# A decode step in fp32: weight rows added on DVE instead of multiplied on PE, shorter programs, the last parts of DVE and PE placed in front

## The chip, the cores and the metric

The kernel runs on one core of a Trainium2 chip. The metric is device time in microseconds (us). The engines are called as the profile calls them: PE (TensorE, with PEld for its weight loads), DVE (VectorE), ACT (ScalarE), POOL (GpSimd) and SP (SyncE, which issues nearly all DMAs here). A name with a q (SPq, PEq) is that engine's sequencer.

## The reference

One token passes through attention over a cache and a gated feed-forward layer, side by side; both results are added to the input. All is float32.

```python
# x (1,1,576); k_cache, v_cache (1,32,16384,128); wq (576,4096); wo (4096,576)
# w_gate, w_up (576,4608); w_down (4608,576)
xn = _layernorm(x)
q = xn @ wq                                  # 32 heads of 128
p = softmax(einsum(q, k_cache) * 128**-0.5)  # per head, over 16384 keys
attn = concat_heads(p @ v_cache) @ wo
h = gelu(xn @ w_gate) * (xn @ w_up)
out = x + attn + h @ w_down
```

## The kernel before

The keys and values of one head are one tile each, 128 partitions x 16384 floats (8.39 MB): partition p holds 128 keys of 128 floats. SBUF holds three such slots: two for K (`kt`, used by even and odd heads) and one for V (`vt`). The weights use the same slots before the heads start and w_down and wo after they end.

`Plan` keeps one list of operations for each engine (`q`). `op` adds one with the semaphores that it waits for, and on DVE, ACT and POOL each operation also waits for the one before it on its engine; `dma` adds a load with its own semaphore; `call` adds a function that writes its instructions itself, which is how loops get in. `emit` writes an engine's list in order, and leaves out waits that an earlier one covers. `take` waits for a semaphore and lowers it again. The order on each engine is the order of the calls in `plan`.

1. x is normalised on one partition and spread over 128 partitions by five small matmuls (L206, L207): partition p gets entries 4p to 4p+3 of xn (`xp`), and the last 64 entries go to two partitions each (`xt`).
2. `wide` (L214) multiplies on PE: the weight rows are the moving operand, `xnb` (xn repeated 32 times) the stationary one. wq takes 40 matmuls, gate and up 60 each. `select` (L237) picks on DVE, for each partition, the columns that belong to it out of the PSUM result, by a product with a mask and a reduction: `qsel` for q, `gu` for gate and up. The gelu (L264 to L269) runs on DVE with one tanh on ACT and gives `hT`.
3. For each of 32 heads: PE spreads the head's q to all partitions (L287), ACT copies it to `qb`; DVE multiplies the K tile with it in place (`products`, L308) and sums over 128 floats (`sums`, L312), takes the maximum through PE (L315 to L317); ACT does the exponentials (L347); PE multiplies them with the V tile in 32 matmuls (L296); ACT and PE gather the result (L349, L301, L351). The first two heads of DVE stand ahead of its loop, the first K tile in two halves.
4. SP issues the loads one by one from a list of 62 (`load_k`, `load_v`): a K load waits for DVE's sums of the head two before (`s_kf`), a V load for PE's use of the V before (`s_vf`). The first K loads wait for PE to be done with gate and up (`done`).
5. `down` (L378) adds the 36 rows of w_down on DVE into `wacc`: 28 (`wd0`) and 5 (`AHEAD`) before the softmax sums are gathered to `oT` (L400 to L406), 3 after. Of wo's 32 rows DVE adds 8 (`ON_DVE`), PE multiplies 18 into `acc` and the last 6 into `fin` (`out_rows`, L413); `part` = `acc` + `wacc` is summed over partitions into `fin` too, which began with x (L419). Each of the last seven rows of wo is a load of its own.

Of the kernel before, what the change touches and what calls it, by code (L numbers as in the profile page):

```python
# [24 lines left out]
FQ = DF // 4  # L25
WT = HD // P
CUT = ((0, 11), (11, 22), (22, 32))
# [5 lines left out]
ON_DVE = range(8)  # L33
AHEAD = 5
LAST = 6


class Plan:
# [26 lines left out]

    def call(self, e, fn):
        self.q[e].append((None, fn, None, 0))

    def emit(self, e, g, seen, ops):
        for deps, fn, sig, by in ops:  # L70
            if deps is None:
                fn(g)
                continue
            need = {}
            for s, n in (d for d in deps if d):
                if n > max(seen.get(s.name, 0), need.get(s.name, (s, 0))[1]):
                    need[s.name] = s, n
            for k, (s, n) in need.items():
                g.wait_ge(s, n)
                seen[k] = n  # L80
            made = fn(g)
            if made is not None:
                made.then_inc(sig, by)

    def run(self, ahead):
        seen = {e: {} for e in self.NAMES}
        for e, n in ahead.items():
            self.emit(e, getattr(self.nc, self.NAMES[e]), seen[e], self.q[e][:n])
        with self.nc.Block(no_gpsimd_drain=True) as block:
            for e, name in self.NAMES.items():  # L90
                getattr(block, name)(lambda g, e=e: self.emit(e, g, seen[e], self.q[e][ahead.get(e, 0) :]))
# [12 lines left out]
def plan(nc, pl, x, k_cache, v_cache, wq, wo, wg, wu, wd, out):  # L104
# [31 lines left out]
    xnb, xtb = small("xnb", [P, DJ, 32]), small("xtb", [P, 2, 32])  # L136
# [7 lines left out]
    tmp = small("tmp", [P, 32 * FT])  # L144
    over = place["tmp"]
    xn, xd = small("xn", [1, D], over), small("xd", [1, D - DM, 2], over + 4 * D)
    t1, th, t2 = (small(f"t{i}", [P, FT], over + 160 * i) for i in range(3))
# [4 lines left out]
    A, B, C = 0, SLOT, 2 * SLOT  # L152
    wqm, wqt = big("wqm", DJ * HD, A), big("wqt", HD // 2, B)
    gm, gt = big("gm", DJ * DF, B + 8192), big("gt", DF // 2, B + 8192 + 16 * DF)
    ua, ub, ut = big("ua", 2 * DF, B + 8192 + 18 * DF), big("ub", 2 * DF, A), big("ut", DF // 2, A + 8 * DF)
# [9 lines left out]
    pqs, pg, pu = banks(("pqs", 2), ("pg", 3), ("pu", 3))  # L165
    po, pqb, pt, pb, pc, acc, fin = banks(("po", 1), ("pqb", 1), ("pt", 1), ("pb", 1), ("pc", 1), ("acc", 2), ("fin", 1))
    px = pu[:, 0, :]
# [41 lines left out]
    k_xnb = op("dve", lambda g: g.tensor_copy(xnb, xp[:, :DJ].unsqueeze(2).to_broadcast([P, DJ, 32])), k)  # L209
    k = op("dve", lambda g: g.tensor_scalar(xt, par, xp[:, DJ:], None, op0=ALU.mult), k, c_par)  # L210
    k_x = op("dve", lambda g: g.tensor_copy(xtb, xt.unsqueeze(2).to_broadcast([P, 2, 32])), k)


    def wide(dst, b, cols, pieces, t, tcols):  # L214
        n = cols[1] - cols[0]
        k = None
        for j in range(DJ + 1):
            for i in range(4):
                o = dst[32 * i : 32 * i + 32, b, :n]
                if j < DJ:  # L220
                    w, dep = pieces[j]
                    c = i * tcols
                    args = xnb[:, j, :], w[:, c + cols[0] : c + cols[1]]
                else:
                    w, dep = t
                    c = (i % 2) * tcols
                    args = xtb[:, i // 2, :], w[:, c + cols[0] : c + cols[1]]
                k = op("pe", lambda g, o=o, a=args, j=j: g.matmul(o, *a, start=j == 0, stop=j == DJ), dep, k_x)  # L228
        return k

    rows = [(wqm[:, j * HD : (j + 1) * HD], d_q[0]) for j in range(DJ)]
    for b in range(2):
        k_q = wide(pqs, b, (512 * b, 512 * b + 512), rows, (wqt, d_q[1]), HD // 4)
    d_ub = dma("sp", ub, main["u"][:, 2 * DF :], k_q)
    d_ut = dma("sp", ut, tail["u"], k_q)

    def select(view, dst, r):  # L237
        tv = tmp[:, : r * dst.shape[-1]].rearrange("p (r t) -> p r t", r=r)
        k = None
        for lo, hi, src, dep in view:  # L240
            k = op("dve", lambda g, lo=lo, hi=hi, src=src: g.tensor_mul(  # L241
                tv[:, lo:hi, :], src.rearrange("p (r t) -> p r t", r=hi - lo),
                m32[:, lo:hi].unsqueeze(2).to_broadcast([P, hi - lo, dst.shape[-1]])), dep, c_m32)
        return op("dve", lambda g: g.tensor_reduce(dst, tv.rearrange("p r t -> p t r"), axis=AX.X, op=ALU.add), k)

    k_qs = select([(0, 8, pqs.rearrange("p b f -> p (b f)"), k_q)], qsel, 8)

    gp = [(gm[:, j * DF : (j + 1) * DF], d_g[j // 2]) for j in range(DJ)]
    up = [(ua[:, :DF], d_ua), (ua[:, DF:], d_ua), (ub[:, :DF], d_ub), (ub[:, DF:], d_ub)]
    done = []  # L250
    for i, (dst, pieces, t) in enumerate(((pg, gp, (gt, d_g[2])), (pu, up, (ut, d_ut)))):
        view = []
        for b, (lo, hi) in enumerate(CUT):
            k = wide(dst, b, (FT * lo, FT * hi), pieces, t, FQ)
            view.append((lo, hi, dst[:, b, : FT * (hi - lo)], k))
        done.append(k)
        k_f = select(view, gu[:, i, :], 32)

    for z in (po, acc, fin):
# [3 lines left out]
    g_, u_ = gu[:, 0], gu[:, 1]  # L263
    k = op("dve", lambda g: g.tensor_mul(t1, g_, g_), k_f)  # L264
    k = op("dve", lambda g: g.tensor_scalar(t1, t1, 0.044715, 1.0, op0=ALU.mult, op1=ALU.add), k)
    k = op("dve", lambda g: g.tensor_mul(t1, t1, g_), k)
    k = op("act", lambda g: g.activation(th, t1, AF.Tanh, scale=0.7978845608028654), k)
    k = op("dve", lambda g: g.scalar_tensor_tensor(t2, th, 1.0, g_, op0=ALU.add, op1=ALU.mult), k)
    k_h = op("dve", lambda g: g.scalar_tensor_tensor(hT, t2, 0.5, u_, op0=ALU.mult, op1=ALU.mult), k)  # L269


    c_h = op("dve", lambda g: g.memset(hcol, 0.0))
    c_h = op("dve", lambda g: g.tensor_copy(hcol[:, :H].rearrange("p (q r) -> p q r", q=4),
                                            ident.rearrange("p (q r) -> p q r", q=4)[:, :, : H // 4]), i1)
# [4 lines left out]
    k = op("act", lambda g: pick(g, 0), c_h)  # L279
    k_pq0 = op("pe", lambda g: g.matmul(pqb[:, 0, :DH], hsel, qsel, start=True, stop=True), k, k_qs)  # L280
    op("act", lambda g: g.activation(qb[0], pqb[:, 0, :DH], AF.Copy), k_pq0, sig=s_qb)
    op("act", lambda g: pick(g, 1), sig=s_hs)
# [77 lines left out]
    def load_v(h):  # L360
        dma("sp", vt, vv[h], (s_vf, h) if h else done[1], sem=s_v)

    dma("sp", kt[0][:, : N // 2 * DH], kv[0][:, : N // 2 * DH], done[0], sem=s_kh)
    dma("sp", kt[0][:, N // 2 * DH :], kv[0][:, N // 2 * DH :], sem=s_k[0])
    load_k(1, done[1])
    for h in range(H - 2):
        load_v(h)
        load_k(h + 2, (s_kf, h + 1))
    load_v(H - 2)
    d_wd0 = dma("sp", wd0, wdv[:, : WD1 * D], (s_kf, H - 1))  # L370
    load_v(H - 1)
    d_wd1 = dma("sp", wd1, wdv[:, WD1 * D :], (s_kf, H))
    k_o = s_ol, H


    o_sum = wacc.rearrange("p a f -> p (a f)")

    def down(lo, hi, w, dep, k):  # L378
        for t in range(lo, hi):
            r, c = w[:, (t - lo) * D : (t - lo + 1) * D], hT[:, t : t + 1]  # L380
            if t == 0:
                k = op("dve", lambda g, r=r, c=c: g.tensor_scalar(o_sum, r, c, None, op0=ALU.mult), dep, k_h)  # L382
            else:
                k = op("dve", lambda g, r=r, c=c: g.scalar_tensor_tensor(o_sum, r, c, o_sum, op0=ALU.mult, op1=ALU.add), dep, k)  # L384
# [3 lines left out]
    k_w1 = down(WD1, WD1 + AHEAD, wd1, d_wd1, k_w0)  # L388
    d_wo, lo = [], 0
    for n in WO_CUTS:  # L390
        w, base, dep = (wo0, 0, (s_kf, H)) if lo < WO1 else (wo1, WO1, k_w0)
# [27 lines left out]
    out_rows(0, ones[:1, :1], xrow, (k_o,), True, False, fin)  # L419
# [44 lines left out]
```

## Time and profile before

| | |
|---|---|
| time, median of 3 runs | 1364.9 us (1364.34 to 1365.13) |
| the profiled execution's own time | 1364.51 us |
| its span, first to last instruction | 1362.7 us |
| mean granted TensorE clock | 0.634 |
| bytes read from HBM | 587.60 MB |

The page of the profile gives busy times of the engines, DMA queues and the costliest groups of instructions. A row of a group reads: line, engine, operation, output<-inputs, form, count | busy us, mean ns of one | idle time before them and what ended it. A row of the timeline reads: start us, us, engine, line, operation, count, and in brackets the idle time before it with its releaser. A row of the windows gives for a stretch the busy us and instructions of PE, PEld, DVE, ACT and POOL, then the granted clock, the busy share of the DMA engines and GB/s. Queues q8 and q14 of kind "instruction" bring the engines' own code.

### The profile page before, as it was taken

How to read it: one execution, taken by the hardware profiler on the slowest of the kernel's cores; microseconds unless marked ns; L12 is line 12 of the kernel's file. 1: busy time of each engine (PE TensorE's matmuls, PEld its weight loads, DVE VectorE, ACT ScalarE, POOL GpSimd, SP SyncE). 2: the span in 40 equal slices, each digit the busy share in tenths (PEclk: the TensorE clock that was granted, in tenths of full speed). 3: DMA queues.
4: the chain of work that ended last, by engine and by line, in shares of the span. 5: the costliest groups of instructions: out<-in, count | busy, mean ns of one | idle time of the engine just before them, and what ended most of it. 6: DMA issues, size and time to landing. Idle time of an engine off the chain costs nothing. (4 is left out here: it accounts for less than half of the span.)

```text
span 1362.7 us, 7234 instructions
## 1 busy us (share of the span) xinstructions
PE 421.6 (31%) x2904; PEld 130.8 (10%) x2904; DVE 1176.6 (86%) x214; ACT 65.3 (5%) x232; POOL 0.7 (0%) x6
## 2 busy tenths in 40 slices
PE   3430233333212333323222333332113333332227
PEld 1110010011000111100000111100001111010001
DVE  1249999999998888899888888998888888988886
ACT  0000000000000000000000000000000000000000
POOL 0000000000000000000000000000000000000000
PEclk9765666666556666665566666665566666665568
DMA  9999999999999999999999999999999999999998
GB/s 399 433 439 431 437 441 439 431 433 431 433 435 431 435 441 437 435 433 431 433 433 433 431 441 441 435 431 433 431 435 433 431 441 439 437 431 433 430 434 347
DMA packets 12682, 587.69 MB, mean 431 GB/s; under 512 B 1410, under 2 KB 1410, under 8 KB 2564
## 3 DMA queue, kind: packets, MB, share of 16 engines
q1 hardware_dynamic: 12674, 587.60, 99.6%
q8 instruction: 4, 0.07, 0.0%
q14 instruction: 2, 0.02, 0.0%
q10 hardware_dynamic: 2, 0.00, 0.0%
HBM read 587.60 MB, written 0.00 MB: 431 GB/s over the span
## 5 line engine op out<-in xcount | busy, mean ns | idle before, releaser
L296 PE MATMUL po<-vt,pe 128*4 128x512 f32 x2048 | 292.9, 736 | 599.9 <-PEq L95 599.9
L308 DVE TENSOR_TENSOR kb<-kb,qb 128x16384 f32<-128x16384 f32 (+1 forms) x17 | 275.8, 16221 | 32.2 <-DVEq L95 32.1
L308 DVE TENSOR_TENSOR ka<-ka,qb 128x16384 f32<-128x16384 f32 x16 | 275.6, 17225 | 31.8 <-DVEq L95 31.8
L312 DVE TENSOR_REDUCE sc<-ka 128x128 f32<-128x16384 f32 x16 | 275.5, 17220 | 2.3
L312 DVE TENSOR_REDUCE sc<-kb 128x128 f32<-128x16384 f32 x16 | 275.5, 17220 | 2.3
L296 PEld LDWEIGHTS po<-vt,pe 128*4 128x4 f32 x2048 | 56.6, 99 | 809.1 <-issue 809.1
L289 PE MATMUL pt<-ident,pm 128*1 128x128 f32 x32 | 11.9, 372 | 235.0 <-PEq L95 235.0
L349 ACT ACTIVATE o<-po 128x512 f32<-128x512 f32 x32 | 19.1, 597 | 866.6 <-ACTq L95 866.6
L301 PE MATMUL pc<-m,o 128*128 128x1 f32 x256 | 32.8, 249 | 28.9 <-PEq L95 28.9
L301 PEld LDWEIGHTS pc<-m,o 128*128 128x128 f32 x256 | 31.0, 191 | 57.7 <-issue 57.7
L384 DVE SCALAR_TENSOR_TENSOR wacc<-wd,hT,wacc 128x576 f32<-128x576 f32 x35 | 28.7, 819 | 2.4 <-DMA wd<-in_B_w_down_dram 1.3
L317 DVE TENSOR_REDUCE nm<-pt 1x1 f32<-1x128 f32 x32 | 8.9, 279 | 21.5 <-DVEq L95 21.5
L289 PEld LDWEIGHTS pt<-ident,pm 128*1 128x1 f32 x32 | 2.5, 79 | 240.3 <-issue 240.3
L291 PE MATMUL pb<-nm,ones 1*128 1x1 f32 x64 | 17.7, 343 | 18.5 <-PEq L95 18.5
L241 DVE TENSOR_TENSOR tmp<-pqs,m 128x1024 f32<-128x1024 f32 x1 | 1.2, 1223 | 25.6 <-PE pqs L228 25.6
L241 DVE TENSOR_TENSOR tmp<-pu,m 128x396 f32<-128x396 f32 (+1 forms) x3 | 1.7, 557 | 22.0 <-PE pu L228 22.0
L241 DVE TENSOR_TENSOR tmp<-pg,m 128x396 f32<-128x396 f32 (+1 forms) x3 | 1.7, 558 | 20.3 <-PE pg L228 20.3
L291 PEld LDWEIGHTS pb<-nm,ones 1*128 1x128 f32 x64 | 15.9, 306 | 27.9 <-issue 27.9
L345 ACT ACTIVATE nb<-pb 128x1 f32<-128x1 f32 x32 | 5.5, 171 | 266.1 <-ACTq L95 266.1
L315 DVE TENSOR_REDUCE pm<-sc 128x1 f32<-128x128 f32 x32 | 9.2, 286 | 7.6 <-DVEq L95 7.6
L287 PE MATMUL pqb<-qsel,hsel 128*128 128x128 f32 x64 | 15.3, 321 | 0.7 <-PEq L95 0.7
L228 PE MATMUL pg<-gm,xnb 128*32 128x396 f32 (+1 forms) x96 | 11.1, 607 | 11.7 <-DMA gm<-in_B_w_gate_dram 11.7
(82 smaller groups left out, 146.4 us busy)
## 6 DMA issues: line engine op xcount, KB each, us to landing
gm<-in_B_w_gate_dram SPq DMA_DIRECT2D x2, 4608.0 KB, 41.0
kb<-in_A_k_cache_dram SPq DMA_DIRECT2D x2, 4096.0 KB, 31.3
wd<-in_B_w_down_dram SPq DMA_DIRECT2D x1, 8064.0 KB, 42.0
ua<-in_B_w_up_dram SPq DMA_DIRECT2D x1, 4608.0 KB, 58.7
ub<-in_B_w_up_dram SPq DMA_DIRECT2D x1, 4608.0 KB, 38.8
wo<-in_A_wo_dram SPq DMA_DIRECT2D x3, 1152.0 KB, 37.4
wd<-in_B_w_down_dram SPq DMA_DIRECT2D x1, 2304.0 KB, 28.1
wo<-in_A_wo_dram SPq DMA_DIRECT2D x1, 2304.0 KB, 32.8
```

Of the source, the lines that this page charges most:

```text
L228: k = op("pe", lambda g, o=o, a=args, j=j: g.matmul(o, *a, start=j == 0, stop=j == DJ), dep, k_x)
L287: g.matmul(pqb[:, 0, :DH], hsel, qsel, start=True, stop=True).then_inc(s_pq, 1)
L289: g.transpose(pt[:1, 0, :P], pm, ident).then_inc(s_pt, 1)
L291: g.matmul(pb[:, 0, :1], ones[:1, :], nm, start=True, stop=True).then_inc(s_pb, 1)
L296: m = g.matmul(po[q : q + 4, 0, :], pe[:, k : k + 4], vt[:, k * DH : (k + 4) * DH], start=k < 16, stop=k >= N - 16)
L301: m = g.matmul(pc[:, 0, :1], o4[:, j * DH : (j + 1) * DH], m32[:, j : j + 1], start=j == 0, stop=j == 3)
L308: g.tensor_mul(kd, kd, qb[i].unsqueeze(1).to_broadcast([P, n[1] - n[0], DH])).then_inc(s_d, 1)
L312: g.tensor_reduce(sc[i], kt[i].rearrange("p (n d) -> p n d", d=DH), axis=AX.X, op=ALU.add).then_inc(s_d, 1)
L315: g.tensor_reduce(pm, sc[i], axis=AX.X, op=ALU.max).then_inc(s_pm, 1)
L317: g.tensor_reduce(nm, pt[:1, 0, :P], axis=AX.X, op=ALU.max, negate=True).then_inc(s_nm, 1)
L349: g.activation(o4, po[:, 0, :], AF.Copy).then_inc(s_o4, 1)
L384: k = op("dve", lambda g, r=r, c=c: g.scalar_tensor_tensor(o_sum, r, c, o_sum, op0=ALU.mult, op1=ALU.add), dep, k)
```

## The change

- **Weights.** `wide` goes. `rows` scales and adds on DVE, in each partition, the four weight rows of that partition and its half row of the tail (`tails`), in place in the weight's own tile and at the end into `both`. PE then only sums over partitions, with `ones` as the stationary operand: 12 matmuls for each of q, gate and up in a loop of three (`sums` on PE), which also spreads the first q of the heads.
- **Selection and gelu** move from DVE to POOL: ACT copies the sums from PSUM to `tmp`, POOL multiplies with the mask and halves the columns by adds until one is left. The copy for gate waits for POOL's and ACT's work on q, the copy for up (`c_u`) for POOL's gelu. POOL also clears `wacc` and puts x into it.
- **Loads.** Each weight comes as first rows, tail, remaining rows. The up loads wait for all of q on DVE (`q_k`), the first K for all of gate (`g_k`), the second K for the last-but-one add of up (`u_k`), the first V for `c_u`. Places in SBUF are changed to match.
- **SP** issues K of heads 2 to 31 and V of heads 1 to 30 from a loop of 15 with the head from a register.
- **The end.** All 36 rows of w_down are added before `oT`; DVE takes 12 rows of wo, PE 14 into `acc`; `part` goes into `fin` one row later.
- **Where the code stands.** The lists of DVE and PE are cut by `late` ahead of the last part. `both` writes a loop of two passes whose body has the last part first, run in pass 1, and all that is ahead of it second, run in pass 0.

```diff
-ON_DVE = range(8)
-AHEAD = 5
+ON_DVE = range(12)
+SEL = 396
...
+    def both(self, e, g, ops):
+        if e not in self.cut:
+            return self.emit(g, ops)
+        with g.Fori(0, 2) as i:
+            i = i.val.handles[0]
+            with g.If_eq(i, 1):
+                self.emit(g, ops[self.cut[e] :])
+            with g.If_eq(i, 0):
+                if e == "dve":
+                    g.addr_align(128, offset=100, max_nops=0)
+                self.emit(g, ops[: self.cut[e]])
...
+    d_q = [dma("sp", q0, main["q"][:, :HD]), dma("sp", qt, tail["q"]), dma("sp", q123, main["q"][:, HD:])]
+    d_g = [dma("sp", gw[0], main["g"][:, : 2 * DF]), dma("sp", gt, tail["g"]), dma("sp", gw[1], main["g"][:, 2 * DF :])]
...
+    def add(out, w, c, into, *deps):
+        return op("dve", lambda g: g.scalar_tensor_tensor(out, w, c, into, op0=ALU.mult, op1=ALU.add), *deps)
...
+    def rows(r, t, d, parts, *deps):
+        s, pads = r[0], []
+        op("dve", lambda g, s=s: g.tensor_scalar(s, s, xp[:, :1], None, op0=ALU.mult), d[0], k_x)
+        if d[1] is d[0]:
+            add(s, r[1], xp[:, 1:2], s)
+            tails(s, t, d[-1])
+        else:
+            tails(s, t, d[-1])
+            k = add(r[1], r[1], xp[:, 1:2], s, d[1])
+            s = r[1]
...
+        k_s = add(r[2], r[2], xp[:, 2:3], s, d[2])
+        v = [u.rearrange("p (i c) -> p i c", i=4) for u in (r[3], r[2])]
+        for lo, hi, to in parts:
+            k = add(bv[:, :, to : to + hi - lo], v[0][:, :, lo:hi], xp[:, 3:4], v[1][:, :, lo:hi], *deps)
+        pl.then("dve", [s_r], k, *pads[-1:])
+        return k_s, k
+
+    def sums(g):
+        with g.Fori(0, 3):
+            take(g, s_h0)
+            g.matmul(pqb[:, 0, :DH], hsel, qsel, start=True, stop=True).then_inc(s_q0, 1)
+            take(g, s_r)
+            for b in range(3):
+                for i in range(4):
+                    m = g.matmul(pw[32 * i : 32 * i + 32, b, :SEL], ones[:, :32], bv[:, i, b * SEL : (b + 1) * SEL], start=True, stop=True)
+            m.then_inc(s_w, 1)
...
+    def select(dst, c, r, n, *deps):
+        k = op("act", lambda g: g.activation(sel[:, : 3 * c].rearrange("p (b c) -> p b c", b=3), pw[:, :, :c], AF.Copy), (s_w, n), *deps)
+        v = sel[:, : r * dst.shape[-1]].rearrange("p (r t) -> p r t", r=r)
+        k_ = op("pool", lambda g, r=r: g.tensor_mul(v, v, m32[:, :r].unsqueeze(2).to_broadcast([P, r, dst.shape[-1]])), k, c_m32)
+        while r > 1:
+            r //= 2
+            o = v[:, :r, :] if r > 1 else dst.unsqueeze(1)
+            k_ = op("pool", lambda g, o=o, r=r: g.tensor_tensor(o, v[:, :r, :], v[:, r : 2 * r, :], op=ALU.add), k_)
+        return k, k_
...
+    def on_sp(g):
+        with g.Fori(0, H // 2 - 1) as m:
+            for i in range(2):
+                take(g, s_kf)
+                g.dma_start(kt[i], two[0][i, bass.ds(m + 1, 1)].rearrange("o p f -> (o p) f")).then_inc(s_k[i], 16)
+                take(g, s_vf)
+                v = two[1][1, bass.ds(m, 1)] if i == 0 else two[1][0, bass.ds(m + 1, 1)]
+                g.dma_start(vt, v.rearrange("o p f -> (o p) f")).then_inc(s_v, 16)
...
-    k_w1 = down(WD1, WD1 + AHEAD, wd1, d_wd1, k_w0)
+    k_w1 = down(WD1, FT, wd1, d_wd1, k_w0)
...
-    out_rows(0, ones[:1, :1], xrow, (k_o,), True, False, fin)
```

More of the change, by code (lines that the diff above doesn't have):

```diff
@@ L24 @@
 FT = DF // P
-FQ = DF // 4
 WT = HD // P
-CUT = ((0, 11), (11, 22), (22, 32))
 S0 = 32512
@@ L64, in dma, with then, late, needs @@
         return self.op(e, lambda g: g.dma_start(out, in_), *deps, sig=sem, by=16)
+    def then(self, e, sems, *deps):
+        self.q[e].append((deps, lambda g: [g.sem_inc(s, 1) for s in sems], None, 0))
     def call(self, e, fn):
         self.q[e].append((None, fn, None, 0))
[L69 to L73, printed above, removed]
+    def late(self, e):
+        self.cut[e] = len(self.q[e])
+    def needs(self, e):
+        seen = {}
+        for deps, *rest in self.q[e]:
@@ L74, in emit @@
             need = {}
-            for s, n in (d for d in deps if d):
+            for s, n in (d for d in deps or () if d):
                 if n > max(seen.get(s.name, 0), need.get(s.name, (s, 0))[1]):
                     need[s.name] = s, n
-            for k, (s, n) in need.items():
-                g.wait_ge(s, n)
-                seen[k] = n
+            seen |= {k: n for k, (_, n) in need.items()}
+            yield list(need.values()), *rest
+    def emit(self, g, ops):
+        for need, fn, sig, by in ops:
+            for d in need:
+                g.wait_ge(*d)
@@ L81, in emit @@
             made = fn(g)
-            if made is not None:
+            if sig is not None and made is not None:
                 made.then_inc(sig, by)
+    def both(self, e, g, ops):
[9 more added lines that the diff above has]
+                self.emit(g, ops[: self.cut[e]])
@@ L85, in run @@
     def run(self, ahead):
-        seen = {e: {} for e in self.NAMES}
+        ops = {e: list(self.needs(e)) for e in self.NAMES}
         for e, n in ahead.items():
-            self.emit(e, getattr(self.nc, self.NAMES[e]), seen[e], self.q[e][:n])
+            self.emit(getattr(self.nc, self.NAMES[e]), ops[e][:n])
+            ops[e] = ops[e][n:]
         with self.nc.Block(no_gpsimd_drain=True) as block:
             for e, name in self.NAMES.items():
-                getattr(block, name)(lambda g, e=e: self.emit(e, g, seen[e], self.q[e][ahead.get(e, 0) :]))
+                getattr(block, name)(lambda g, e=e: self.both(e, g, ops[e]))
@@ L143, in plan @@
     gu, hT = small("gu", [P, 2, FT]), small("hT", [P, FT])
-    tmp = small("tmp", [P, 32 * FT])
+    sel = small("tmp", [P, 3 * SEL])
     over = place["tmp"]
     xn, xd = small("xn", [1, D], over), small("xd", [1, D - DM, 2], over + 4 * D)
-    t1, th, t2 = (small(f"t{i}", [P, FT], over + 160 * i) for i in range(3))
+    t1, th, t2 = (small(f"t{i}", [P, FT]) for i in range(3))
     wacc, part = small("wacc", [P, 2, HALF], over), small("part", [P, 2, HALF], over + 4 * D)
@@ L163, in banks @@
             return [s.enter_context(nc.psum_tensor(n, [P, b, 512], F32)).ap() for n, b in shapes]
-    pqs, pg, pu = banks(("pqs", 2), ("pg", 3), ("pu", 3))
-    po, pqb, pt, pb, pc, acc, fin = banks(("po", 1), ("pqb", 1), ("pt", 1), ("pb", 1), ("pc", 1), ("acc", 2), ("fin", 1))
-    px = pu[:, 0, :]
+    (pw,) = banks(("pw", 3))
+    pt, pb, pc, pqb, po, acc, fin = banks(("pt", 1), ("pb", 1), ("pc", 1), ("pqb", 1), ("po", 1), ("acc", 2), ("fin", 1))
+    px = pc[:, 0, :]
     s_hs, s_pm, s_nm, s_p, s_o4, s_v = (pl.sem(n) for n in ("hs", "pm", "nm", "p", "o4", "v"))
@@ L208, in plan @@
     k = op("dve", lambda g: g.tensor_copy(xp, px[:, : DJ + 1]), k)
[L209 to L257, printed above, removed]
@@ L259, in plan @@
-    for z in (po, acc, fin):
-        op("dve", lambda g, z=z: g.memset(z, 0.0))
[L263 to L268, printed above, removed]
@@ L274, in plan @@
                                             ident.rearrange("p (q r) -> p q r", q=4)[:, :, : H // 4]), i1)
+    for z in (po, acc, fin):
+        op("dve", lambda g, z=z: g.memset(z, 0.0))
+    bv = both.rearrange("p (i c) -> p i c", i=4)
+    s_r, s_w, s_h0, s_q0 = (pl.sem(n) for n in ("r", "w", "h0", "q0"))
+    op("pool", lambda g: g.memset(qsel, 0.0))
+    op("pool", lambda g: g.memset(hsel, 0.0), sig=s_h0)
+    def add(out, w, c, into, *deps):
+        return op("dve", lambda g: g.scalar_tensor_tensor(out, w, c, into, op0=ALU.mult, op1=ALU.add), *deps)
@@ L276, in pick @@
+    qr = [q0] + [q123[:, j * HD : (j + 1) * HD] for j in range(DJ - 1)]
+    _, q_k = rows(qr, qt, [d_q[0], d_q[2], d_q[2], d_q[2], d_q[1]], [(384 * b, min(384 * b + 384, HD // 4), SEL * b) for b in range(3)])
+    d_u = [dma("sp", uw[0], main["u"][:, : 2 * DF], q_k), dma("sp", ut, tail["u"]), dma("sp", uw[1], main["u"][:, 2 * DF :])]
+    c_q, k = select(qsel, 384, 8, 1)
     def pick(g, h):
         return g.activation(hsel, hcol[:, bass.ds(h, 1)].to_broadcast([P, P]), AF.Copy)
-    k = op("act", lambda g: pick(g, 0), c_h)
@@ L280, in plan, with four @@
-    k_pq0 = op("pe", lambda g: g.matmul(pqb[:, 0, :DH], hsel, qsel, start=True, stop=True), k, k_qs)
-    op("act", lambda g: g.activation(qb[0], pqb[:, 0, :DH], AF.Copy), k_pq0, sig=s_qb)
-    op("act", lambda g: pick(g, 1), sig=s_hs)
+    op("act", lambda g: pick(g, 0), k, c_h, sig=s_h0)
+    k = op("act", lambda g: g.activation(qb[0], pqb[:, 0, :DH], AF.Copy), (s_q0, 2))
+    pl.then("act", [s_qb, s_h0], k)
+    def four(w, t, d, *deps):
+        return rows([u[:, j * DF : (j + 1) * DF] for u in w for j in range(2)], t, [d[0], d[0], d[2], d[2], d[1]],
+                    [(0, DF // 4, 0)], *deps)
@@ new lines, in plan @@
+    _, g_k = four(gw, gt, d_g, c_q)
+    c_g, k_g = select(gu[:, 0], SEL, 32, 2, k)
+    u_k, _ = four(uw, ut, d_u, c_g)
+    g_, u_ = gu[:, 0], gu[:, 1]
+    k = op("pool", lambda g: g.tensor_mul(t1, g_, g_), k_g)
+    k = op("pool", lambda g: g.tensor_scalar(t1, t1, 0.044715, 1.0, op0=ALU.mult, op1=ALU.add), k)
+    k = op("pool", lambda g: g.tensor_mul(t1, t1, g_), k)
+    k = op("act", lambda g: g.activation(th, t1, AF.Tanh, scale=0.7978845608028654), k)
+    k = op("pool", lambda g: g.tensor_scalar(t2, th, 0.5, 0.5, op0=ALU.mult, op1=ALU.add), k)
@@ L284, in on_pe @@
+    k_t = op("pool", lambda g: g.tensor_mul(t2, t2, g_), k)
+    c_u, k = select(u_, SEL, 32, 3, k_t)
+    op("act", lambda g: pick(g, 1), (s_q0, 3), sig=s_hs)
+    k = op("pool", lambda g: g.tensor_mul(hT, t2, u_), k)
+    k = op("pool", lambda g: g.memset(wacc, 0.0), k)
+    k_h = op("pool", lambda g: g.tensor_copy(wacc[:1].rearrange("p a f -> p (a f)"), xrow), k)
     def on_pe(g):
@@ L360, in load_v @@
     def load_v(h):
-        dma("sp", vt, vv[h], (s_vf, h) if h else done[1], sem=s_v)
-    dma("sp", kt[0][:, : N // 2 * DH], kv[0][:, : N // 2 * DH], done[0], sem=s_kh)
+        dma("sp", vt, vv[h], (s_vf, 1) if h else c_u, sem=s_v)
+    dma("sp", kt[0][:, : N // 2 * DH], kv[0][:, : N // 2 * DH], g_k, sem=s_kh)
     dma("sp", kt[0][:, N // 2 * DH :], kv[0][:, N // 2 * DH :], sem=s_k[0])
[L365 to L370, printed above, removed]
+    load_k(1, u_k)
+    load_v(0)
+    two = [c.rearrange("(m t) p f -> t m p f", t=2) for c in (kv, vv)]
+    def on_sp(g):
+        with g.Fori(0, H // 2 - 1) as m:
+            for i in range(2):
+                take(g, s_kf)
[3 more added lines that the diff above has]
+                g.dma_start(vt, v.rearrange("o p f -> (o p) f")).then_inc(s_v, 16)
+    pl.call("sp", on_sp)
+    d_wd0 = dma("sp", wd0, wdv[:, : WD1 * D], (s_kf, 1))
     load_v(H - 1)
-    d_wd1 = dma("sp", wd1, wdv[:, WD1 * D :], (s_kf, H))
+    d_wd1 = dma("sp", wd1, wdv[:, WD1 * D :], (s_kf, 2))
     k_o = s_ol, H
+    pl.late("dve")
+    pl.late("pe")
     o_sum = wacc.rearrange("p a f -> p (a f)")
```

41 lines of the change are left out of this document (20 added, 21 removed).

## The prediction

> **What bounds the kernel now.** I read the page first, then windows at both ends of the span, then the timeline where tiles land. The page:
>
> ```profile
> span 1362.7 us, 7234 instructions
> ## 1 busy us (share of the span) xinstructions
> PE 421.6 (31%) x2904; PEld 130.8 (10%) x2904; DVE 1176.6 (86%) x214; ACT 65.3 (5%) x232; POOL 0.7 (0%) x6
> ...
> DMA packets 12682, 587.69 MB, mean 431 GB/s; under 512 B 1410, under 2 KB 1410, under 8 KB 2564
> ...
> q8 instruction: 4, 0.07, 0.0%
> q14 instruction: 2, 0.02, 0.0%
> ```
>
> DVE at 86% looks like a bound and is not one: what never pauses is the DMA stream. Whether it pauses at its ends is seen in windows of 2 us (the last two columns are the busy share of the sixteen DMA engines, above 1 where packets are booked at their end, and GB/s):
>
> ```profile
> 0.00:2.00 2.00, 0.00 (x0) 0.00 (x0) 0.52 (x3) 0.53 (x1) 0.70 (x6) 1.00 0.20 67
> ...
> 1354.00:1356.00 2.00, 2.00 (x16) 0.62 (x14) 0.20 (x1) 0.00 (x0) 0.00 (x0) 1.00 1.05 411
> 1356.00:1358.00 2.00, 2.00 (x19) 0.52 (x16) 0.55 (x1) 0.00 (x0) 0.00 (x0) 1.00 0.70 263
> 1358.00:1360.00 2.00, 1.54 (x10) 0.18 (x8) 0.27 (x1) 0.27 (x1) 0.00 (x0) 1.00 0.05 20
> ```
>
> In the first 2 us all sixteen engines did 0.4 us of work, and after 1358 only 0.1: the stream runs from less than 2 us to 1358. Its pace is read from PE, which begins each head's V product when that V has landed:
>
> ```profile
> 133.92 8.48 PE L296 MATMUL po<-vt,pe 128*4 128x512 f32 x64 [3.38 <-PEq L95]
> ```
>
> ```profile
> 1254.37 9.74 PE L296 MATMUL po<-vt,pe 128*4 128x512 f32 x64 [21.02 <-PEq L95]
> ```
>
> 29 heads lie between: 1120.45 / 29 = 38.64 us for one K and one V tile of 8.39 MB each, 434 GB/s, 19.3 us a tile. All 587.69 MB at that pace are 1354 us of the 1362.7. The change moves the same bytes, so it can win only what the stream loses at its ends, and it loses at once if a load is issued after the stream has run dry.
>
> **The parts, one by one.** *Weights on DVE.* 160 of PE's matmuls and the selections of DVE go; DVE scales and adds whole rows in place instead. The prices:
>
> ```profile
> L308 DVE TENSOR_TENSOR ka<-ka,qb 128x16384 f32<-128x16384 f32 x16 | 275.6, 17225 | 31.8 <-DVEq L95 31.8
> L312 DVE TENSOR_REDUCE sc<-ka 128x128 f32<-128x16384 f32 x16 | 275.5, 17220 | 2.3
> ...
> L384 DVE SCALAR_TENSOR_TENSOR wacc<-wd,hT,wacc 128x576 f32<-128x576 f32 x35 | 28.7, 819 | 2.4 <-DMA wd<-in_B_w_down_dram 1.3
> L308 DVE TENSOR_TENSOR kb<-kb,qb 128x8192 f32<-128x8192 f32 x2 | 17.4, 8692 | 1.9 <-DVEq L95 1.9
> ...
> L382 DVE TENSOR_SCALAR wacc<-wd,hT 128x576 f32<-128x576 f32 x1 | 0.5, 521 | 2.0 <-DMA wd<-in_B_w_down_dram 2.0
> ```
>
> From 8192 to 16384 elements the product grows by 8533 ns, 1.042 ns an element. At that slope L384 has 819 - 600 = 219 ns fixed, and L382 (one tensor in) 0.52 ns an element. An add over 4096 elements is then 4.49 us, over 4608 5.02, over 2304 2.62; a scaling of 4608 is 2.64. The other bound is L384's whole price by length, 1.42 ns an element. I take the slope, because the long instructions here are nearest to L308.
>
> When data lands:
>
> ```profile
> 23.04 5.89 PE L228 MATMUL pqs<-wqm,xnb 128*32 128x512 f32 x32 [15.35 <-DMA wqm<-in_A_wq_dram]
> ```
>
> ```profile
> 75.84 1.55 PE L228 MATMUL pu<-ut,xtb 128*32 128x396 f32 x8
> ```
>
> wq without its tail is in at 23.0, with it (1.05 MB) at 25.5. All three weights are in at 75.8; backwards at 434 GB/s the new order (rows 0-1, tail, rows 2-3) has up's second half at 75.8, its tail at 65.0, its first half at 62.2, gate's second half at 51.4. DVE after 25.5: two adds of 4096, then 1536, 1536 and 1024 columns into `both`, with 0.03 between: 39.5, when the up loads are issued, 11 us ahead of need (the gate loads hold the stream until 51.4). Gate: 2.64 + 5.02 + 2 x 2.62 + 2 x 5.02 and gaps, done at 62.6: first K issued. Up: its last-but-one add needs the half of 75.8 and ends at 80.9: second K issued; the last add at 85.9. Then 12 matmuls on PE and ACT's copy out of PSUM, from these:
>
> ```profile
> 48.62 2.87 PE L228 MATMUL pg<-gm,xnb 128*32 128x396 f32 x16 [8.05 <-DMA gm<-in_B_w_gate_dram]
> ```
>
> ```profile
> L349 ACT ACTIVATE o<-po 128x512 f32<-128x512 f32 x32 | 19.1, 597 | 866.6 <-ACTq L95 866.6
> ```
>
> x16 records are 8 matmuls, so 12 take 4.3; 1188 columns take at most 1.4. The first V is issued at 85.9 + 4.3 + 1.4 + some 0.4 of hand-overs = 92. Products of the first K in halves (8.69 each, the second half lands at 75.8 + 19.3 = 95.2) and its sums (17.2) end at 121.2: third K issued. Before, these issues stood here:
>
> ```profile
> 84.66 0.33 SPq L64 DMA_DIRECT2D ka<-in_A_k_cache_dram  x1
> 85.03 0.43 SPq L64 DMA_DIRECT2D vt<-in_A_v_cache_dram  x1
> 128.54 0.33 SPq L64 DMA_DIRECT2D kb<-in_A_k_cache_dram  x1
> ```
>
> The deadlines follow from V landing at 133.9: third K before 133, first V before 133.9 - 19.3 - some 1 from issue to flow (the first window) = 113, second K before 94, first K before 75. Cover is 12, 21, 13 and 12 us. So the weights' part costs nothing, hidden under the stream; the third K even gains 7 us of cover, which buys nothing.
>
> *K and V in a loop on SP.* Two register instructions go ahead of an issue of 0.33 us. The trace has no such issue; bounds are nothing and a second 0.43. V's next load leaves about 10 us after the last landed, while a K tile of 19.3 us is in the queue: hidden, and without that cover 0.43 a load, 60 loads, 26 us.
>
> *DVE's last part.* All eight adds of the second w_down piece now stand ahead of the softmax sums, twelve wo rows behind them instead of eight:
>
> ```profile
> 1336.75 4.23 DVE L384 SCALAR_TENSOR_TENSOR wacc<-wd,hT,wacc 128x576 f32<-128x576 f32 x5 [1.25 <-DMA wd<-in_B_w_down_dram]
> ...
> 1342.36 0.36 DVE L400 RECIPROCAL rl<-pqb 128x32 f32<-128x32 f32 x1 [1.38 <-PE pqb L399]
> ...
> 1343.95 0.37 DVE L406 TENSOR_REDUCE oT<-ot 128x32 f32<-128x128 f32 x1
> ...
> 1355.80 0.76 DVE L429 TENSOR_TENSOR part<-acc,wacc 128x576 f32<-128x576 f32 x1 [2.02 <-PE acc L416]
> ```
>
> Eight adds at 0.85 end at 1343.5, so the reciprocal is 1.2 us later; from its start to the end of oT (L406) it is 1.96, and twelve adds are 10.2: 1355.7. `part` stands where it stood, 1355.7 against 1355.80. The end is the last piece of wo:
>
> ```profile
> 1359.00 0.70 PE fin L416 x4
> ```
>
> *Code in front.* In the listing of the program PE has 259 matmuls before and 101 after, four instructions each (two loads, two passes): 1036 and 404. Four q8 packets for 1036 are one per 259, of 17 KB; for 404 I expect one or two, early. A packet of 17 KB at 434/16 GB/s holds one of sixteen engines for 0.65 us, and every load waits for its slowest engine. What this can be worth is in the windows: after 1356 there are 2 x (0.70 + 0.05) = 1.5 us of work for all sixteen, which spread evenly would end at 1357.5; PE got the last piece at 1359.0. The 1.5 between hold the notice to PE too. Bounds of the gain: 0 (the slowest engine carried no packet) and 1.5; I take 0.9, one packet and a little.
>
> **Sum.** The profiled run took 1364.51, 1.81 outside its span and 0.39 under the median of 1364.9. 1364.51 - 0.9 = 1363.6, on the median's scale 1364.0.
>
> **The rivals.** *POOL is kept from SBUF by DVE, and the first V is late (slower).* The selections and the gelu go to POOL, beside a DVE that is now busy without a gap from 25 to 121. V's load waits for ACT's third copy, which waits for POOL's eleven steps since the second. If POOL may not read while DVE reads two tensors, each step waits for the end of an add or a product. POOL's price:
>
> ```profile
> L186 POOL TENSOR_SCALAR_AFFINE_SELECT ident<-ident 128x128 f32<-128x128 f32 x1 | 0.3, 292 | 0.2 <-POOL ident L185 0.2
> ```
>
> 0.292 for 128 elements is 2.3 ns each at most; DVE's 1.04 is the lower bound. First case, one POOL step behind each DVE instruction: ACT's second copy ends at 71 to 73, five steps follow five adds of up, the sixth the first half of the product (99 to 105), the seventh the second half (108 to 113), the other four run beside the sums, which have one tensor in: V's issue at 111 to 117. Second case, POOL served only where DVE waits or reduces: the second copy waits for the first selection, so DVE stops ahead of up's last add at 81, POOL's four steps and the copy take until 90 to 93, add and products until 113 to 115, the eleven steps until 117 to 123: V's issue at 119 to 125. It decides from 113 on, and each microsecond past it is lost: nothing to 4 in the first case, 6 to 12 in the second; I price it at 8, 1372, with 1364 and 1376 as its ends. For it: the new overlap is dense. Against: this trace shows no such block, since POOL stops at 1.7 us, and without one POOL is done by 77. [...]
>
> *The jump back stalls PE.* After the last head PE branches to code in front. If it must be fetched, oT is late: 1.2 us are covered by DVE's adds and some 0.5 by the rows before `part`. The nearest price is a small load behind a full queue:
>
> ```profile
> wo<-in_A_wo_dram SPq DMA_DIRECT2D x7, 288.0 KB, 18.2
> ```
>
> Bounds are 0 and 18 us; q8 is a queue of its own, so I take 3, which gives 1363.9 + 1.3 = about 1365.3. Against: PE branches back 31 times in its head loop, and four packets in all were fetched. [...]
>
> *The adds cost 1.42 ns an element.* Second K at 97 and third K at 138, 5 past its deadline: 1369.
>
> *Nothing gained.* The uneven end has another cause: 1364.9.
>
> **How the numbers follow.** Forecast 0.55, nothing gained 0.11, POOL 0.25, jump 0.06, dear adds 0.03. The forecast's own range is 1362.8 to 1364.8; the range given goes up to 1370, which takes in the dear adds and the mild end of POOL's case and leaves out some 0.16 above and 0.03 below. Faster by over 0.2% (2.7 us, about what a measurement of this kernel can tell from no change) needs more than the ends have to give: 0.03. Within: 0.52 + 0.11 + 0.05 = 0.68. Slower: 0.25 + 0.03 + 0.01 = 0.29.
>
> **What would show it.** Right: one or two q8 packets, no window below a share of about 0.9 from 4 to 1356 us, first V issued near 92 and third K near 121, PE's last wo piece near 1358. Wrong: a POOL step of many microseconds and an issue of V past 113 with a hole in the stream; a gap on PE between the last L344 and L450; adds of 4608 longer than 5.3 us.

## The result, and the profile after

| | before | after |
|---|---|---|
| median (lowest to highest, runs) | 1364.59 us (1364.34 to 1365.13, 19) | 1367.20 us (1366.78 to 1367.83, 19) |
| span of the profiled execution | 1362.7 us | 1364.8 us |
| ratio, 95% interval | | 1.0019 [1.0012, 1.0026] |

The change costs 2.6 us; 1364.0 was forecast. The page after:

```profile
PE 394.6 (29%) x2640; PEld 123.8 (9%) x2640; DVE 1240.5 (91%) x221; ACT 68.9 (5%) x235; POOL 63.3 (5%) x35
...
q8 instruction: 1, 0.02, 0.0%
```

PE lost 264 matmul records and 27 us, DVE gained 64 us, POOL went from 0.7 to 63.3. None of this bounds the kernel. The stream does: q1's packets take 99.5% of the span of the sixteen DMA engines. The windows of 2 us show where it stops:

```profile
110.00:112.00 2.00, 0.00 (x0) 0.00 (x0) 1.85 (x2) 0.17 (x1) 1.80 (x1) 0.50 0.53 229
112.00:114.00 2.00, 0.00 (x0) 0.00 (x0) 2.00 (x1) 1.23 (x2) 0.48 (x2) 0.50 0.00 0
114.00:116.00 2.00, 0.77 (x2) 0.50 (x2) 2.00 (x1) 0.78 (x3) 1.96 (x1) 0.50 1.53 524
116.00:118.00 2.00, 0.00 (x0) 0.00 (x0) 2.00 (x1) 0.00 (x0) 1.84 (x3) 0.50 0.00 0
```

The kernel before has no such windows there:

```profile
112.00:114.00 2.00, 0.00 (x0) 0.00 (x0) 2.00 (x1) 0.00 (x0) 0.00 (x0) 0.50 1.06 459
114.00:116.00 2.00, 0.00 (x0) 0.00 (x0) 2.00 (x1) 0.00 (x0) 0.00 (x0) 0.50 1.21 524
116.00:118.00 2.00, 0.00 (x0) 0.00 (x0) 2.00 (x1) 0.00 (x0) 0.00 (x0) 0.50 1.21 524
```

From 112 to 118 the sixteen DMA engines were given 1.53 x 2 = 3.1 of 6 us of work, against 7.0 before (a packet counts whole in the window in which it starts, not at its end as the prediction reads it). Packet by packet, they stand idle for 2.6 us on average between 112.1 and 115.5: there was nothing in the queue. The timeline of the same place names what the queue waited for. From POOL's selection of gate on:

```profile
72.50 4.45 POOL L285 TENSOR_TENSOR tmp<-tmp,m 128x1152 f32<-128x1152 f32 x1 [10.17 <-ACT tmp L283]
...
75.07 7.96 DVE L243 SCALAR_TENSOR_TENSOR u<-ut,xt,u 128x2304 f32<-128x2304 f32 x2
77.03 16.82 POOL L289 TENSOR_TENSOR tmp<-tmp 128x576 f32<-128x576 f32 x4
83.14 5.36 DVE L243 SCALAR_TENSOR_TENSOR u<-u,xp,u 128x4608 f32<-128x4608 f32 x1
88.52 0.33 SPq L62 DMA_DIRECT2D ka<-in_A_k_cache_dram  x1
88.60 5.06 DVE L243 SCALAR_TENSOR_TENSOR both<-u,xp 128x4608 f32<-128x4608 f32 x1
...
94.03 8.71 DVE L351 TENSOR_TENSOR kb<-kb,qb 128x8192 f32<-128x8192 f32 x1 [0.37 <-DVEq L115]
94.27 8.57 POOL L314 TENSOR_TENSOR t<-gu 128x36 f32<-128x36 f32 x1
...
102.93 0.22 POOL L315 TENSOR_SCALAR t<-t 128x36 f32<-128x36 f32 x1
102.99 8.69 DVE L351 TENSOR_TENSOR kb<-kb,qb 128x8192 f32<-128x8192 f32 x1 [0.26 <-DVEq L115]
103.23 8.57 POOL L316 TENSOR_TENSOR t<-t,gu 128x36 f32<-128x36 f32 x1
111.83 17.22 DVE L355 TENSOR_REDUCE sc<-kb 128x128 f32<-128x16384 f32 x1
...
112.46 0.26 POOL L319 TENSOR_TENSOR t<-t,gu 128x36 f32<-128x36 f32 x1
112.80 1.16 ACT L283 ACTIVATE tmp<-pw 128x1188 f32<-128x1188 f32 x1 [0.73 <-POOL t L319]
113.99 0.33 SPq L62 DMA_DIRECT2D vt<-in_A_v_cache_dram  x1
```

L314, L316 and L319 are the same kind of step, a product over 36 elements. Beside DVE's sums (L355) it takes 0.26 us; beside a half of its product (L351) it takes 8.57 and ends with it. So POOL's gelu ends at 112.7, ACT's copy of up's sums (`c_u`) at 113.96, and the first V is issued at 113.99. Its tile reaches PE 1.92 us later than before (133.92), and the end is late by about as much: DVE's last copy starts at 1361.77 against 1359.73.

```profile
135.84 6.44 PE L339 MATMUL po<-vt,pe 128*4 128x512 f32 x44 [4.62 <-PEq L115]
```

The end of the changed kernel, and the last row of the kernel before:

```profile
1358.13 0.76 DVE L477 TENSOR_TENSOR part<-acc,wacc 128x576 f32<-128x576 f32 x1
1361.77 0.45 DVE L480 COPY osb<-fin 1x288 f32<-1x288 f32 x1 [2.88 <-PE fin L465]
```

```profile
1359.73 0.45 DVE L432 COPY osb<-fin 1x288 f32<-1x288 f32 x1 [3.17 <-PE fin L416]
```

### The profile page after: what moved, and what is told of

It reads as the page before. It is cut to its first block, busy times and chain, and to the rows that moved or that the text cites. A ratio compares the mean times of both kernels' runs of the same rounds, so it can differ in the third digit from the quotient of the medians.

```text
span 1364.8 us, 7006 instructions
## 1 busy us (share of the span) xinstructions
PE 394.6 (29%) x2640; PEld 123.8 (9%) x2640; DVE 1240.5 (91%) x221; ACT 68.9 (5%) x235; POOL 63.3 (5%) x35
## 2 busy tenths in 40 slices
DMA packets 12823, 587.64 MB, mean 431 GB/s; under 512 B 1426, under 2 KB 1426, under 8 KB 2580
## 3 DMA queue, kind: packets, MB, share of 16 engines
q1 hardware_dynamic: 12818, 587.60, 99.5%
## 5 line engine op out<-in xcount | busy, mean ns | idle before, releaser
L351 DVE TENSOR_TENSOR ka<-ka,qb 128x16384 f32<-128x16384 f32 x16 | 275.6, 17225 | 32.4 <-DVEq L115 32.4
L351 DVE TENSOR_TENSOR kb<-kb,qb 128x16384 f32<-128x16384 f32 (+1 forms) x17 | 275.8, 16222 | 31.6 <-DVEq L115 31.6
L355 DVE TENSOR_REDUCE sc<-kb 128x128 f32<-128x16384 f32 x16 | 275.5, 17220 | 2.3
L355 DVE TENSOR_REDUCE sc<-ka 128x128 f32<-128x16384 f32 x16 | 275.5, 17220 | 2.3
L277 PE MATMUL pw<-both,ones 128*32 128x396 f32 x72 | 12.2, 848 | 58.2 <-PEq L115 58.2
L289 POOL TENSOR_TENSOR tmp<-tmp 128x576 f32<-128x576 f32 (+5 forms) x10 | 26.0, 2597 | 0.8
L390 ACT ACTIVATE pe<-sc,nb 128x128 f32<-128x128 f32 x32 | 12.8, 401 | 6.1 <-ACTq L115 6.1
L243 DVE SCALAR_TENSOR_TENSOR q<-q,xp,q 128x4096 f32<-128x4096 f32 x1 | 4.5, 4484 | 7.9 <-DMA q<-in_A_wq_dram 7.9
```

Of the source, the lines that this page charges most:

```text
L243: return op("dve", lambda g: g.scalar_tensor_tensor(out, w, c, into, op0=ALU.mult, op1=ALU.add), *deps)
L289: k_ = op("pool", lambda g, o=o, r=r: g.tensor_tensor(o, v[:, :r, :], v[:, r : 2 * r, :], op=ALU.add), k_)
L351: g.tensor_mul(kd, kd, qb[i].unsqueeze(1).to_broadcast([P, n[1] - n[0], DH])).then_inc(s_d, 1)
L355: g.tensor_reduce(sc[i], kt[i].rearrange("p (n d) -> p n d", d=DH), axis=AX.X, op=ALU.add).then_inc(s_d, 1)
L390: g.activation(pe, sc[i], AF.Exp, bias=nb, scale=SCALE, accum_out=ls[:, bass.ds(h, 1)]).then_inc(s_p, 1)
```

## The experiments

The theory: DVE's instructions that read two tensors keep POOL out, POOL's gelu ends with the second half product, V is issued too late. The first rival: the 2.6 us come from the code in front or from the end, and the hole is harmless. All ratios are against the kernel before, run beside each experiment (1364.54 us in the first four, 1364.62 in the last three).

**1. V's issue freed by order alone (x2_copy_ahead).** ACT's copy of up's sums goes ahead of the tanh and waits only for gate's selection; POOL and DVE do the same work.

```diff
+    c_u = copy(SEL, 3, k_g)
     k = op("act", lambda g: g.activation(th, t1, AF.Tanh, scale=0.7978845608028654), k)
...
-    c_u, k = select(u_, SEL, 32, 3, k_t)
+    _, k = select(u_, SEL, 32, 3, k=c_u)
```

> The changed kernel, with ACT's third copy out of PSUM placed ahead of its tanh and waiting only for POOL's selection of gate (done at 94), not for the gelu. Theory (late V): POOL's steps stay as long (8.57 each beside the products), V is nevertheless issued near 99.5, no hole, 1365.5 (1364.9 to 1366.0). Rival (blocked POOL steps cost in another way, by slowing DVE): 1367, since DVE and POOL overlap as before. Rival (code in front, loop on SP): 1367.

Measured: 1364.92 us, ratio 1.0004 [0.9995, 1.0013]: level with before. The timeline of this kernel:

```profile
94.06 8.57 POOL L318 TENSOR_TENSOR t<-gu 128x36 f32<-128x36 f32 x1
97.91 1.16 ACT L283 ACTIVATE tmp<-pw 128x1188 f32<-128x1188 f32 x1 [25.36 <-PE pw L277]
99.09 0.33 SPq L62 DMA_DIRECT2D vt<-in_A_v_cache_dram  x1
...
103.03 8.57 POOL L320 TENSOR_TENSOR t<-t,gu 128x36 f32<-128x36 f32 x1
```

The stream does not stop:

```profile
112.00:114.00 2.00, 0.76 (x2) 0.50 (x2) 2.00 (x1) 0.74 (x3) 1.84 (x3) 0.50 1.14 492
114.00:116.00 2.00, 0.00 (x0) 0.00 (x0) 2.00 (x1) 0.00 (x0) 1.92 (x2) 0.50 1.13 492
```

POOL is kept out as long as in the changed kernel, but V no longer waits for it, and 2.3 of the 2.6 us are gone. The slow POOL steps cost nothing in themselves; the load behind them did.

**2. POOL let in (x1_product_waits).** DVE's first product waits until the gelu is done (`k_t`).

```diff
+        g.wait_ge(*k_t)
```

> The changed kernel, with DVE's first product made to wait until POOL's gelu is done. Theory (POOL's steps are blocked by DVE instructions that read two tensors, so the first V is issued too late): with DVE idle for some 2 us after up's last add, the two 8.57 us steps shrink to about 0.3 each, V is issued near 99.5 instead of 114.0, no window has a DMA share of 0.00, and the time falls by the hole net of what it evened out, about 1.7, to 1365.5 (1364.9 to 1366.0). Rival (the loss comes from the code in front or from the loop on SP): 1367 or more.

Measured: 1367.08 us, ratio 1.0019 [1.0010, 1.0028], as slow as the change: a miss in the time, and by its number what the rival had forecast. The trace shows another cause than the rival's. Its timeline:

```profile
94.09 0.24 POOL L314 TENSOR_TENSOR t<-gu 128x36 f32<-128x36 f32 x1
...
94.72 0.26 POOL L316 TENSOR_TENSOR t<-t,gu 128x36 f32<-128x36 f32 x1
...
96.04 8.69 DVE L351 TENSOR_TENSOR kb<-kb,qb 128x8192 f32<-128x8192 f32 x1 [2.56 <-DVEq L115]
...
98.67 0.33 SPq L62 DMA_DIRECT2D vt<-in_A_v_cache_dram  x1
...
104.99 10.27 DVE L351 TENSOR_TENSOR kb<-kb,qb 128x8192 f32<-128x8192 f32 x1 [0.26 <-DVEq L115]
106.79 11.57 POOL L289 TENSOR_TENSOR tmp<-tmp 128x576 f32<-128x576 f32 x4
115.41 17.22 DVE L355 TENSOR_REDUCE sc<-kb 128x128 f32<-128x16384 f32 x1
...
133.05 0.34 SPq L417 DMA_DIRECT2D kb<-in_A_k_cache_dram  x1
```

The block itself is confirmed: with DVE idle, the two steps of 8.57 take 0.24 and 0.26, and V leaves at 98.67. But the first product starts 2.0 later, its second half, from 104.99, takes 10.27 in place of 8.69 because POOL's selection of up (its first step ends at 106.71) stands in its way, and the sums end at 132.6: the third K is issued at 133.05 (129.47 in the changed kernel). The hole has moved there:

```profile
130.00:132.00 2.00, 0.00 (x0) 0.00 (x0) 2.00 (x1) 0.00 (x0) 0.00 (x0) 0.50 0.16 66
132.00:134.00 2.00, 0.37 (x1) 0.08 (x1) 1.09 (x3) 0.00 (x0) 0.00 (x0) 0.50 0.00 0
```

My expectation had followed V's wait only, not the next load that DVE's delay makes late.

**3. V later still (x4_v_later).** It waits for the end of POOL's list (`k_h`) in place of `c_u`.

> The changed kernel, with the first V load made to wait for POOL's last step (at 121.5 in the trace) instead of ACT's third copy. Theory (late V, each microsecond past the dry point is lost once): V is issued 7.6 later, at 121.6, the time is 1367.2 + 7.6 = 1374.8 (1374 to 1375.6). Rival (a late V is made up for later, since DVE runs ahead of the stream): less than 1370.

Measured: 1374.61 us, ratio 1.0074 [1.0058, 1.0089]; V issued at 121.54, 7.55 us later than in the changed kernel, time 7.41 longer. The rival, a late V made up for later, is out.

```profile
121.54 0.33 SPq L62 DMA_DIRECT2D vt<-in_A_v_cache_dram  x1
```

Here a microsecond of V's issue past the deadline was a microsecond of the time. Counted back from both kernels by the spans over the 1362.7 of experiment 1 (121.54 - 9.7, 113.99 - 2.1), the deadline lies near 112 in these two kernels.

**4. Without the code in front (x3_no_front).** The two calls of `late` are left out.

> The changed kernel without the cut: DVE's and PE's last parts stand last, in order. Theory (late V): the hole at 112 to 114 stays and the time is 1367.2 within 1; the code packets come at other times. Rival (the loss comes from code fetched in the first microseconds or from the jump back): 1364.5 to 1365.5.

Measured: 1366.44 us, ratio 1.0012 [1.0003, 1.0021], 0.8 less than the changed kernel and within the band of the theory; the rival is out. V is issued at 112.12, 1.87 earlier. That comes from the first weight: q's add, which waits for wq's last rows in both kernels, starts at 25.17 in place of 27.03. For these rows the first of the sixteen DMA engines is done at 24.5 here and at 24.3 in the changed kernel, the last at 24.8 and 26.5. (DVE's first instruction also starts earlier, at 1.05 in place of 2.03 us, but DVE then waits for these rows all the same, 6.77 us here and 7.92 in the changed kernel.)

```profile
25.17 4.48 DVE L243 SCALAR_TENSOR_TENSOR q<-q,xp,q 128x4096 f32<-128x4096 f32 x1 [6.77 <-DMA q<-in_A_wq_dram]
...
112.12 0.33 SPq L62 DMA_DIRECT2D vt<-in_A_v_cache_dram  x1
...
134.19 3.60 PE L339 MATMUL po<-vt,pe 128*4 128x512 f32 x16 [4.83 <-PEq L115]
```

```profile
27.03 4.48 DVE L243 SCALAR_TENSOR_TENSOR q<-q,xp,q 128x4096 f32<-128x4096 f32 x1 [7.92 <-DMA q<-in_A_wq_dram]
```

PE gets V at 134.19, 1.65 earlier. Only part of that arrives at the end; experiment 5 has what speaks to it.

**5. Copy ahead and no code in front (x5_copy_ahead_no_front)**: experiment 1 without the two calls of `late`.

> x2_copy_ahead with the last parts of DVE and PE back at the end of their lists (no pass loop). Without the hole in the stream the time is set by the stream's two ends alone. Theory (the code in front costs at the start what it saves at the end: DVE started at 2.03 us against 1.05 and code packets of 8 and 16 KB came at 5 to 6 us of the span): DVE starts near 1.05, q's first add about 1 to 2 us earlier, some code packets again late, and the time is level with x2_copy_ahead, 1364.9 within 0.5. Rival 1 (late code packets hold the end, as the forecast had it): 0.7 to 1.5 us slower, 1365.6 to 1366.4. Rival 2 (the front only costs): 0.7 to 1.5 us faster, 1363.4 to 1364.2.

Measured: 1364.30 us (1364.12 to 1364.60), ratio 0.9998 [0.9989, 1.0007]. The first rival, that late code packets hold the end, is out: this is the forecast's own term for the code in front, and without that code the kernel is not slower. The time is 0.6 under experiment 1, in the gap between my theory and the second rival, that the front only costs; the two intervals overlap, and this does not settle it. Against experiment 4, which differs in the copy alone, it is 2.1 shorter, so the copy is worth about the same with and without the code in front. Of the 2.1, 1.1 are there when V reaches PE (134.19 against 133.08); where the rest comes from stays open, since the engines of experiment 4 stand idle for only 0.7 us ahead of V, against 2.6 in the changed kernel. The code packets tell a little more. Behind each load stand sixteen packets of 4 bytes (88 loads and 1410 such packets before, 89 and 1426 in the changed kernel), read here as one notice of each DMA engine at the end of its share. The code packets hold up the same engines: in the kernel before, the sixteen notices of wq's rows, at 22, lie within 0.65 us, those of gate's first rows, behind the 16 KB at 34, within 1.88. The table has, from the packets of the traces, the time from the first of the sixteen notices to the last:

```
                           code packets from the first load on     first gate rows   last wo load
before                     16 KB at 34, 67, 139, 1356;                 1.88 us          1.54 us
                           8 KB at 134, 1315
the change                 8 KB at 5, 16 KB at 6, 8 KB at 24           2.23             0.38
1: copy ahead              8 KB at 5, 16 KB at 6, 8 KB at 24           1.84             1.62
4: no front                8 KB at 105, 16 KB at 143                   0.35             1.38
5: copy ahead, no front    8 KB at 105, 16 KB at 141                   0.45             1.31
```

A packet of 16 KB took 0.88 to 0.96 us (0.65 was reckoned), and the spread behind the early ones stayed to the end of the stream: 1.84 and 1.62 in experiment 1. Where the stream had a hole the engines came out of it even: the spread falls from 2.23 to 0.38 in the changed kernel, from 1.95 to 0.50 behind the hole of experiment 2 and from 1.98 to 0.53 behind that of experiment 3. So early code is not shown to be cheaper than late code. That the rest of experiment 4 is lost in this way is argued, not shown: V arrives 1.65 earlier than in the changed kernel, but its 16 KB packet comes after the hole and the last load spreads by 1.38 in place of 0.38, which leaves some 0.65 of the 0.8 measured (the two profiled executions differ by 0.4 only). In the kernel of experiment 5 V arrives 0.79 earlier than in experiment 1, of which 0.6 is left at the end. Its V product, and behind it that of experiment 1:

```profile
133.08 9.29 PE L343 MATMUL po<-vt,pe 128*4 128x512 f32 x60 [3.67 <-PEq L115]
```

```profile
133.87 8.56 PE L343 MATMUL po<-vt,pe 128*4 128x512 f32 x64 [2.84 <-PEq L115]
```

**6. The loop of loads alone (x6_loop_only)**, put into the kernel before.

```diff
+        with g.Fori(0, H // 2 - 1) as m:
...
+                g.dma_start(kt[i], two[0][i, bass.ds(m + 1, 1)].rearrange("o p f -> (o p) f")).then_inc(s_k[i], 16)
```

> The kernel before with SP's loop for the loads of K 2 to 31 and V 1 to 30 alone. Theory (the register instructions on SP are hidden while another tile is in the queue): no hole, the time of the kernel before, 1364.5 within 0.4. Rival (each issue comes some tenths later and the stream thins 60 times): slower by 1 us or more, with windows below a share of 0.95 between 140 and 1300 us.

Measured: 1364.62 us, ratio 1.0 [0.9991, 1.0009]. The loop costs nothing that can be measured; an issue takes 0.34 us in it against 0.33.

**7. The loop and the end (x7_loop_and_end)**, in the kernel before (x still enters `fin` through PE).

```diff
-ON_DVE = range(8)
-AHEAD = 5
+ON_DVE = range(12)
+AHEAD = 8
...
-        if t == WT - LAST + 1:
+        if t == WT - LAST + 2:
```

> x6_loop_only with the last parts of the change: eight w_down rows ahead of the softmax sums, twelve wo rows on DVE, part one row later (x is still added by PE into fin). Theory (DVE's end is hidden under the last wo loads): part starts within 1 us of 1356, the last wo matmuls as in the kernel before, the time 1364.5 within 0.5. Rival (DVE's twelve rows hold the end): part later than 1357.5 and the time 1 to 2 us longer.

Measured: 1364.63 us, ratio 1.0 [0.9991, 1.0009]. `part` starts here:

```profile
1356.52 0.76 DVE L438 TENSOR_TENSOR part<-acc,wacc 128x576 f32<-128x576 f32 x1
```

That is 0.72 later than before (1355.80), and `part` is now wanted one row later. The end costs nothing either.

## Why the prediction was wrong

*The step that failed* is "Cover is 12, 21, 13 and 12 us. So the weights' part costs nothing, hidden under the stream". The 21 us of the first V rested on an issue "near 92", and that on POOL being done by 77. The sum priced POOL's eleven steps as hidden, at their unblocked length; two of them took 8.57 us each, and gate's selection before them lasted from 72.50 to 94.19, where up's, beside the sums, took from 114.04 to 119.83. The issue came at 113.99, 22 us late: the whole cover and more. Experiment 1 splits the 22: with the copy ahead of the gelu the issue stands at 99.09, so 14.9 are the wait for the gelu, and the other 7 come with DVE's late adds (below). It also gives 2.3 of the 2.6 us to this load alone, and experiment 3 shows the slope.

*The rival that held* was "POOL is kept from SBUF by DVE", in its first case: issue at 111 to 117, "nothing to 4" lost. Measured are 113.99 and 2.6. It has one POOL step held by each half of the product and the last ones beside the sums, and so it is, except that a short step more slipped in ahead of each half, so that the two held are the seventh and the ninth in place of the sixth and the seventh. The price it was given, 1372, mixed in the second case, in which DVE is stopped ahead of up's last add; POOL got in between DVE's adds (each of its steps at L289 beside them ends 0.2 to 1.3 us behind one of them), so this did not come about. What spoke against it, that the trace of before shows no block, was no evidence, since POOL did nothing there after 1.7 us.

What was measured is the block itself: POOL's product over 36 elements took 8.57 beside half a product of DVE and 0.26 beside the sums, and DVE's half product 10.27 in place of 8.69 in experiment 2. That it lies at SBUF, as the rival has it, no run shows.

*The block works both ways*, and the forecast left that out for the adds too. Next to POOL's selection of q they took:

```profile
46.76 3.91 POOL L285 TENSOR_TENSOR tmp<-tmp,m 128x1024 f32<-128x1024 f32 x1 [14.23 <-ACT tmp L283]
49.02 7.60 DVE L243 SCALAR_TENSOR_TENSOR g<-gt,xt,g 128x2304 f32<-128x2304 f32 x2
```

2 x 2.62 = 5.24 was forecast, 7.60 measured, and 7.96 for up's two beside the selection of gate. With the late start of q's adds (27.03 against 25.5) this puts the second K's issue at 88.52 where 80.9 was forecast, under its deadline of 94 still, and the third K's at 129.47 where 121 was forecast: the cover that was to grow by 7 us shrank by 1. The add of 5.36 us at 83.14 passes the forecast's mark for dear adds, 5.3, but it stands among POOL's steps.

*The price of the adds* was right where POOL is away: 4.48 us for 4096 elements, 5.02 for 4608, 2.62 for the scaling (4.49, 5.02, 2.64 forecast). The groups of lines of the changed kernel:

```profile
L243 DVE SCALAR_TENSOR_TENSOR g<-g,xp 128x4608 f32<-128x4608 f32 x1 | 5.0, 5020 | 0.0
...
L243 DVE SCALAR_TENSOR_TENSOR q<-q,xp 128x4096 f32<-128x4096 f32 x1 | 4.5, 4485 | 0.0
...
L253 DVE TENSOR_SCALAR g<-g,xp 128x4608 f32<-128x4608 f32 x1 | 2.6, 2622 | 0.2 <-DVE both L243 0.2
```

*The deadlines* were too late. V's, 113, lay near 112: it was reckoned from the last engine of the stream, but the sixteen notices of the second K's load run from 112.1 to 114.3 in the changed kernel, so the first engines were dry before 113. From issue to PE's first use it took 135.84 - 113.99 = 21.85 us, where 19.3 + 1 was reckoned. The third K's, 133, lay near 131 if all that experiment 2 loses is put down to it (133.05 - 1.9, by the spans 1364.6 and 1362.7).

*The 0.9 us of the code in front* did not come. One q8 packet was right; that an early packet leaves the end even was not. With the hole away (experiment 1) the last load spreads over 1.62 us against 1.54 before, and the time is level; without the code in front (experiment 5) it is not longer either.

*No jump stall.* PE's first matmul in the front code follows the last of the heads at once:

```profile
1343.14 1.02 PE L344 MATMUL pc<-m,o 128*128 128x1 f32 x8 [0.90 <-PEq L115]
...
1344.02 0.39 PE L450 MATMUL pqb<-ls,ones 128*128 128x32 f32 x2
```

Whether a jump to code that must be fetched first would stall PE is not tested by this: no q8 packet followed the one at 6 us.

*SP's loop and DVE's end* were priced at nothing and cost nothing (experiments 6 and 7), though DVE's end came at its edge: `part` was forecast at 1355.7 and stood at 1356.52 in experiment 7.

What stays open: the 0.4 us between experiment 1 and before, whether experiment 5 gains 0.3, and whether the code in front costs the 0.6 between the two, all less than these runs can tell; and about 1 us of the 2.1 between experiments 4 and 5. No version was found that beats the kernel before by a measurable amount.

## What to carry to other kernels

When work moves to POOL beside a busy DVE, price each of POOL's products and adds, however small, at the length of the DVE product or add it meets (here 8.57 us beside half a product for 36 elements that took 0.26 beside the sums), and follow the chain behind it to the next load. In a kernel bound by its stream, write down for every early load the issue time and the deadline under that pessimistic price; the cover that looks largest may rest on the least certain term. And when a wait is taken off one load, check the next one: experiment 2 only moved the hole.

## What was not expected of the hardware

In the selections POOL came in at every seam between two DVE adds: one step per add, with DVE then late by a little less than that step takes beside the sums (5.24 to 7.60 us for two adds of gate; up's two were late by 1.67 and 1.01 behind steps of 2.13 and 1.40). And a late DMA engine stayed late: sixteen engines that early code packets had pulled apart were so at the end of the stream, 1300 us later (1.84 and 1.62 us in experiment 1), where the stream did not stop; in the changed kernel the hole that cost 2 us of time shrank the spread from 2.23 to 0.38 us.
